# A delta-rule recurrence with an MLP behind it, on one core: the inverse's two PSUM banks lent to the MLP's second product, one weight piece fewer, the last outputs on two queues, and a new planning table

## The chip, the cores and the metric

The kernel runs on one core of a Trainium2 chip. Its time is the device time of one execution in microseconds (us). Of the kernel before, three timed runs are shown, from 648.24 to 648.99 us, with a median of 648.69. One more execution was recorded by the profiler. The engines are named as in the profile: PE multiplies matrices, DVE, ACT and POOL (GpSimd) work on elements, SP issues most transfers. PSUM is the memory that PE writes its products to; here it is eight banks of 512 float32 values in each of 128 partitions.

## The reference

```python
# r, k, v, w, a, b: 4 x 8 x 768 x 40, float32; state: 4 x 8 x 40 x 40, zero at first
for t in range(768):
    y[:, :, t] = einsum('bhd,bhde->bhe', r_t, state)
    Sa = einsum('bhde,bhe->bhd', state, a_t)
    state = state * w_t[:, :, None, :] - einsum('bhd,bhe->bhde', Sa, b_t)
    state = state + einsum('bhd,bhe->bhde', v_t, k_t)
x = y.transpose(0, 2, 1, 3).reshape(3072, 320)
out = (((x @ w1) * (x @ w2)) @ w3) @ w_out        # w1, w2: 320 x 1024, w3: 1024 x 1024, w_out: 1024 x 320
```

The four weights are float64. The kernel gets their bits as pairs of 32-bit words.

## The kernel before, in words

**Chunks.** The 768 tokens are cut into 12 chunks of 64. The chunks depend on each other through the state (`SB`) alone. Inside a chunk the recurrence is solved with matrices: the function `scale` (lines 492 to 533) multiplies the inputs by running products of the decay (`scan` L502, `gt` L515, `gi` L519, `xx` L523, `aa` L512), `causal` multiplies them with each other (PE L551) and leaves the 64 x 64 triangles in `JP` and `lm`, and the triangles of all 32 heads are inverted.

**The inverse.** `solve` (from line 571) takes the 32 x 32 blocks on the diagonal. DVE transposes them into the PSUM tile `ab` of 128 x 1024, which is two banks (L604; for the first two chunks, `MERGED`, only half of it), and inverts them there by some forty products and sums (L630 and L634, tags `so.x`). Two transposes put the result into `TDX` (L690 and L693). For the first two chunks two products on PE (`so.m1`, `so.m2`) stand in for a part of that work. `join` (from line 737) makes the block below the diagonal: an inverse product on PE (`jo.mm1`, L753), four copies by ACT into `JP` (L273, the line of the helper `copy`, which all ACT copies have), a second inverse product (`jo.mm2`, L753), and copies into `TT`.

**The state step.** `rec` works on two batches of a chunk at a time (a pair step). All its products have line 840: `zv`, the state product (`rv,SB`), `zn`, three steps with the inverse and flips that transpose the new state. DVE masks `un` between them (L891) and makes the new state `st` (L896) and the output `y` (L900). `pairs` and `tokens` prepare operands (L792, L816), with a mask on POOL (L801).

**The MLP.** `gather` brings `y` into token order by 12 transfers of SP (L915). `mlp` splits it into a high and a low part (`xs`, L940 on ACT and L943 on DVE). Its first product (tag `m.mm1`, L957) gives x @ w1 and x @ w2, 128 matmuls of 256 columns for a chunk, in groups of eight. ACT copies one (`ga`), DVE multiplies it by the other (L971), and the result is split into `gh` (ACT) and `gl` (L974, POOL or DVE). The second product (tag `m.mm2`, L983) multiplies by w3 @ w_out, which was multiplied out at the start: 48 matmuls of 320 columns in two halves of 128 tokens. Each half fills one bank from the pool of six banks that all of PE's products share. ACT copies it to `o`, and two transfers for each half leave by SP (L992).

**The weights.** `convert` turns a piece of 128 x 1024 float64 values into float32: one transfer, `e` (L394), `mf` (L404), its low word (L408), `sg` (L412) on DVE, two steps on ACT, and the output of the conversion (L415) on DVE or POOL, as a table says. There are 17 pieces: 3 of w_out, 8 of w3, 6 of w1 and w2 in three layers of 128 rows. Since 320 is 2 x 128 + 64, the third layer repeats its 64 rows. ACT copies each of these six to the high part of W (`w.hi`), and `w.lo` (L457) makes the low part.

**The order of the work.** All of this goes to a planner, the class `Order`. Each operation is given with a tag, a due time and the buffers that it takes (`SLOTS` says how many of each there are). `place` puts them on the engines one after another by estimated costs (`OPS`) and due times (`P`, `OFF`, `T0`, `T`): of the operations that could start on an engine within `LOOK` of the first, the one with the earliest due time. On PE `STICK` counts against a change of mode, between products of 128, 64 and 32 rows. `ON` says for some tags whether DVE or POOL does them. The result is a fixed order on each engine, with semaphores between them. When an operation runs on the chip depends on these alone.

**The end.** Behind the last chunk a check of the inputs' range sums `stats`, PE multiplies it by ones (L1098, `good`), DVE makes the flag `bad`, and all engines load it (L1102) and branch on it (L1103). The branch isn't taken with these inputs.

Of the kernel before, what the change touches and what calls it, by code (L numbers as in the profile page):

```python
# [19 lines left out]
NCH = S // C  # L20
# [12 lines left out]
SLOTS = dict(fm=4, xx=3, aa=3, lm=4, gi=1, gt=1, ab=1, TDX=1, rv=4, vg=5, un=4, bk=5, hs=2, st=2, y=1, xr=1, JP=2, TT=2, bank=6,  # L33
# [8 lines left out]
ON = dict(aa="dppddpdddppdpppddppppddd", cv="pdddppdddpddddppp",
          gl="dpppdpppddppddpppdddddpppppdpdpdppppddddpppdpppp", ws="pdddpp", xs="ddpddppppdpppdddppddpdpd")
OFF = {"ca.j": -611.218, "ca.js": -295.116, "ca.lm": -409.432, "ca.mask": 322.878, "ca.mm": -196.496, "cv.e":
       -352.619, "cv.exp": -294.308, "cv.f": 875.871, "cv.in": 923.729, "cv.lo": 148.411, "cv.m": -331.453, "cv.out":
       -690.808, "cv.sign": -986.054, "ga": 652.698, "jo.cp1": 176.7, "jo.cp2": 1171.31, "jo.mm1": 500.308, "jo.mm2":
       559.977, "jo.tt": 1216.266, "ld.aa": 255.685, "ld.fm": -308.122, "ld.xx": -220.769, "m.a": -43.748, "m.ab":
       -25.534, "m.gh": -539.967, "m.gl": -14.3, "m.mm1": 97.143, "m.mm2": 289.0, "m.o": 98.802, "m.out": -533.298,
       "m.xh": -105.084, "m.xl": 349.579, "nil": 390.528, "pa.cp": -142.457, "pa.mask": 411.539, "pa.mm": 399.693,
       "pa.rv": 721.462, "pa.v": -32.743, "r.hs": -489.727, "r.n": 318.043, "r.s": -178.475, "r.sb": -189.193, "r.st":  # L50
       490.608, "r.t0": -269.903, "r.t1": 72.728, "r.t2": -860.309, "r.tr": -475.318, "r.u": -459.283, "r.y":
       -480.807, "r.zn": -15.068, "r.zv": -155.411, "sc.aa": 621.487, "sc.chk": -167.343, "sc.exp": 187.27, "sc.gi":
# [59 lines left out]
class Part:  # L112


    def __init__(self, slot, i):
        self.slot, self.i = slot, i

    @property
    def t(self):
        return self.slot.t[:, self.i * NP:(self.i + 1) * NP]  # L120


class Order:

# [7 lines left out]
    def slot(self, pool):  # L135
        return Slot(self, pool)
# [1039 lines left out]
```

## Time and profile before

| what | value |
|---|---|
| three runs, median (lowest to highest) | 648.69 us (648.24 to 648.99) |
| profiled execution: its own time | 643.84 us |
| its span, first to last instruction | 642.1 us |
| mean granted PE clock | 0.984 |
| busy in the span: PE, DVE, ACT, POOL | 88%, 74%, 60%, 29% |
| bytes moved by DMA | 68.23 MB |

The span is shorter than the execution's own time by what lies around the instructions, 1.74 us. A busy time is the sum of an engine's instructions; an idle time is what is left, and the profile names for it the instruction on another engine (the releaser) whose semaphore came last. PE's float32 matmuls appear twice each in the counts of the trace: an order's `x16` is a trace's `x32`. In the names of tiles the trace leaves the buffer's number out; the orders below show it. In 40 slices of 16 us the page shows a granted clock below 0.9 four times: 0.8, 0.6 and 0.8 between 96 and 177 us, and 0.8 in the last.

### The profile page before, as it was taken

What the parts mean: (1) busy time and instruction counts of PE and PEld (TensorE: products, weight loads), DVE (VectorE), ACT (ScalarE), POOL (GpSimd) and SP (SyncE); (2) the same over time, 40 slices, a digit from 0 to 9 for tenths busy, and PEclk for the clock granted to TensorE, in tenths of its full rate; (3) what the DMA queues carried; (4) which work ended last, traced back from release to release, by engine and by line L of the source; (5) the groups of instructions that cost most, each with busy time, mean ns of one, the idle gap of its engine ahead of it and who ended that gap; (6) DMA issues with size and microseconds to landing.
All of it is one profiled execution on the core that took longest, in us unless ns stands there. A gap on an engine that the chain in (4) does not pass through costs nothing.

```text
span 642.1 us, 27039 instructions
## 1 busy us (share of the span) xinstructions
PE 566.2 (88%) x11970; PEld 503.9 (78%) x11970; DVE 473.3 (74%) x849; ACT 382.5 (60%) x825; POOL 184.7 (29%) x230
## 2 busy tenths in 40 slices
PE   1536889867999999999999999998999999999995
PEld 0435767556988988888888889887988898898995
DVE  6799897987949959769589599497595794971220
ACT  6767557686465665755755746657557557354221
POOL 3542414035332413403312115332232242020111
PEclk9999989968999999999999999999999999999998
DMA  8975566535213423523534335235135333210001
GB/s 193 294 225 167 154 212 217 196 87 152 69 29 85 117 69 98 141 48 90 137 80 110 82 79 134 59 96 141 41 93 141 78 83 81 51 37 14 26 21 25
DMA packets 53401, 68.23 MB, mean 106 GB/s; under 512 B 29984, under 2 KB 37664, under 8 KB 51232
## 3 DMA queue, kind: packets, MB, share of 16 engines
q1 hardware_dynamic: 53280, 66.46, 38.3%
q8 instruction: 95, 1.56, 1.0%
q14 instruction: 26, 0.21, 0.1%
HBM read 57.79 MB, written 3.93 MB: 96 GB/s over the span
## 4 chain that ended last, share of the span: by engine, by line
PE 36%; DVE 28%; ACT 17%; DMA 9%; SPq 5%; issue 4%; POOL 0%; ACTq 0%; DVEq 0%
PE bank L957 15%; PE bank L840 9%; ACT JP L273 5%; DVE tmp L630 4%; SPq L915 4%; DMA fm<-in_fmg_dram 4%; PE bank L983 4%; ACT TT L273 3%; PE bank L551 3%; DMA xr<-y 3%; DVE ab L604 2%; PE bank L470 2%; DVE mf L408 2%; DVE ga L971 2%; ACT hs L273 2%
## 5 line engine op out<-in xcount | busy, mean ns | idle before, releaser
L957 PE MATMUL bank<-xs,W 128*128 128x256 f32 x1536 | 208.3, 288 | 2.8 <-ACT o L273 2.8
L957 PEld LDWEIGHTS bank<-xs,W 128*128 128x128 f32 x1536 | 187.8, 189 | 14.1 <-ACT o L273 3.6
L273 ACT ACTIVATE gh<-ga 128x512 fp32r<-128x512 f32 x48 | 30.3, 631 | 94.8 <-DVE ga L971 94.8
L891 DVE TENSOR_TENSOR un<-bank,mask_h 128x416 f32<-128x416 f32 x48 | 28.2, 588 | 73.0 <-PE bank L840 63.9
L974 POOL TENSOR_TENSOR gl<-ga,gh 128x512 fp32r<-128x512 f32 x29 | 37.5, 1292 | 118.3 <-ACT gh L273 92.4
L801 POOL TENSOR_SCALAR_AFFINE_SELECT vg<-vg 64x256 f32<-64x256 f32 x96 | 43.9, 457 | 74.6 <-DVE gl L974 24.0
L983 PE MATMUL bank<-W3h,gh 128*128 128x320 f32 x192 | 63.8, 332 | 0.0
L567 POOL TENSOR_SCALAR_AFFINE_SELECT lm<-lm 64x512 f32<-64x512 f32 x48 | 34.0, 708 | 95.5 <-ACT lm L273 74.7
L983 PE MATMUL bank<-W3l,gh 128*128 128x320 f32 x192 | 59.2, 308 | 0.0
L983 PE MATMUL bank<-W3h,gl 128*128 128x320 f32 x192 | 59.2, 308 | 0.0
L273 ACT ACTIVATE JP<-bank 64x256 f32<-64x256 f32 (+2 forms) x120 | 45.4, 379 | 20.7 <-PE bank L551 19.0
L840 PE MATMUL bank<-hs,TT 64*64 64x104 f32 x768 | 49.8, 269 | 7.3 <-ACT TT L273 5.2
L840 PE MATMUL bank<-un,bk 64*64 64x104 f32 (+1 forms) x768 | 47.9, 266 | 2.8 <-DVE un L891 2.3
L523 POOL TENSOR_TENSOR xx<-xx,gi 112x1024 f32<-112x1024 f32 x12 | 28.5, 2379 | 74.6 <-DVE gi L519 22.9
L971 DVE TENSOR_TENSOR ga<-bank,ga 128x512 f32<-128x512 f32 x48 | 32.7, 681 | 22.3 <-PE bank L957 22.3
L840 PEld LDWEIGHTS bank<-hs,TT 64*64 64x64 f32 x768 | 39.3, 142 | 11.5 <-ACT TT L273 6.0
L840 PE MATMUL bank<-vg,bk 64*64 64x104 f32 (+1 forms) x768 | 47.1, 264 | 0.0
L840 PEld LDWEIGHTS bank<-un,bk 64*64 64x64 f32 (+1 forms) x768 | 37.8, 130 | 8.9 <-DVE un L891 5.6
L551 PE MATMUL bank<-aa,xx 40*64 40x64 f32 x1536 | 32.8, 239 | 10.7 <-POOL xx L523 5.5
L551 PEld LDWEIGHTS bank<-aa,xx 40*64 40x64 f32 x1536 | 30.5, 153 | 12.9 <-POOL xx L523 5.7
L470 PE MATMUL bank<-wof,w3f 128*128 128x320 f32 x128 | 38.0, 453 | 2.4 <-DVE w3f L415 1.5
L273 ACT ACTIVATE ga<-bank 128x512 f32<-128x512 f32 x48 | 28.7, 597 | 16.9 <-PE bank L957 16.3
(120 smaller groups left out, 1245.9 us busy)
## 6 DMA issues: line engine op xcount, KB each, us to landing
rv<-in_rv_dram SPq DMA_DIRECT2D x48, 294.0 KB
xx<-in_fmx_dram SPq DMA_DIRECT2D x24, 448.0 KB
raw<-in_w3t_dram SPq DMA_DIRECT2D x8, 1024.0 KB
raw<-in_w_dram SPq DMA_DIRECT2D x6, 1024.0 KB
fm<-in_fmg_dram SPq DMA_DIRECT2D x24, 227.5 KB
aa<-in_fma_dram SPq DMA_DIRECT2D x24, 224.0 KB
vg<-in_vt_dram SPq DMA_DIRECT2D x48, 80.0 KB
out_dram<-o SPq DMA_DIRECT2D x48, 80.0 KB
```

What stands on the lines that cost most here:

```text
L273: act.activation(out_, in_, AF.Copy, scale=scale)
L470: pe.matmul(out=pt.t[:, 0:DM], lhsT=w[:, j], rhs=wof[:, j], start=(j == 0), stop=(j == NJ - 1))
L523: e.tensor_tensor(out=X, in0=X, in1=gi.t.unsqueeze(2).to_broadcast([ROWS, 2 * NP, 2, C]), op=ALU.mult)
L551: pe.matmul(out=bank(s)[64 * z:64 * z + 64, i, p], lhsT=X[r, p, z], rhs=aa[i].t[r, p], start=True, stop=True)
L567: op("ca.mask", due + 6, lambda q=q: pool.affine_select(out=lm.t[q], in_=lm.t[q], pattern=[[0, 2 * NP], [1, C]], compare_op=ALU.is_gt, fil ...
L801: op("pa.mask", due + 2, lambda q=q, vg=vg: pool.affine_select(out=vg.t[q, :, 0:C], in_=vg.t[q, :, 0:C], pattern=[[0, NP], [1, C]], compar ...
L840: pe.matmul(out=out_(ab ^ z, p), lhsT=left(ab, ab ^ x, p), rhs=right(ab ^ x, p), start=start and p == 0, stop=True, skip_group_check=True)
L891: dve.tensor_tensor(out=un[i].t, in0=view(hp[i]), in1=mask_h.unsqueeze(1).to_broadcast([128, NP, N]), op=ALU.mult)
L957: pe.matmul(out=pt.t[:, TOK * x:TOK * x + TOK], lhsT=WT[k][:, cs], rhs=xs.t[:, z], start=(n == 0), stop=(n == 7))
L971: op("m.ab", t, lambda a=a, pt=pt: dve.tensor_tensor(out=a.t, in0=wide(pt), in1=a.t, op=ALU.mult), r=[pt], w=[a])
L974: both(("gl", c % NCH * 4 + j // 2), "m.gl", t + 1, lambda e, a=a, j=j: e.tensor_tensor(out=gl.t[:, j:j + 2], in0=a.t, in1=gh.t[:, j:j + 2 ...
L983: pe.matmul(out=pt.t[:, 0:DM], lhsT=l.t[:, j, ts], rhs=W3[r][:, j], start=(j == 0 and n == 0), stop=(j == NJ - 1 and n == 2))
```

## The change

There are four edits.

1. The pool `ab` with one buffer becomes the pool `xb` with two, which are the two halves of `ab`, one bank each. An inverse takes both (for the first two chunks one). The second product of the MLP takes one for each of its halves, in place of a bank from the pool of six.
2. The third layer of w1 and w2, 64 rows, comes as one piece of 128 x 1024 (`wc`: w1's rows above w2's) in place of two pieces with the rows repeated. There are 16 pieces. The two `w.hi` and the two `w.lo` of that layer work on 64 rows each, and both `w.lo` are on DVE.
3. In the last chunk the second transfer of each half (`m.oa`) is issued by ACT, in place of SP.
4. The planner's tables have new numbers: `T0`, `T`, `P`, `ON`, `OFF`, some costs in `OPS` (with a delay for cold transfers and one for their landing, which `place` now adds), `LOOK` and `STICK`.

```diff
-SLOTS = dict(fm=4, xx=3, aa=3, lm=4, gi=1, gt=1, ab=1, TDX=1, rv=4, vg=5, un=4, bk=5, hs=2, st=2, y=1, xr=1, JP=2, TT=2, bank=6,
+SLOTS = dict(fm=4, xx=3, aa=3, lm=4, gi=1, gt=1, xb=2, TDX=1, rv=4, vg=5, un=4, bk=5, hs=2, st=2, y=1, xr=1, JP=2, TT=2, bank=6,
...
-T0, T = 449.562, 122.639
+T0, T = 555.384, 101.503
...
-FLIGHT, QUEUE, STICK = 1.9, 8, 34.913
+FLIGHT, QUEUE, STICK = 1.9, 8, 4.365
...
+class Whole:
+
+
+    def __init__(self, t):
+        self.t = t
...
+    tiles["xb"] = [tiles["ab"][0][:, 512 * i:512 * i + 512] for i in range(2)]
...
-    pieces = iter(range(17))
+    pieces = iter(range(16))
...
-            for f in range(2 * DFF // CW):
+            for f in range(2 * DFF // CW if k < 2 else 1):
                 cs = slice(CW * f, CW * f + CW)
-                mf = convert(w12[k * 128:k * 128 + 128, cs], None, due)
-                n = (0, 1, 4)[k]
-                rows = slice(64, 128) if k == 2 else slice(0, 128)
+                mf = convert(w12[k * 128:k * 128 + 128, cs] if k < 2 else wc, None, due)
                 over = ["conv"] if k == 0 else ["conv", "reg2"]
-
-                def f1(mf=mf, n=n, cs=cs):
-                    copy(WT[n][:, cs], mf.t)
-
-                def f2(e, mf=mf, n=n, rows=rows, k=k, cs=cs):
-                    e.tensor_tensor(out=WT[2 + k][rows, cs], in0=mf.t[rows], in1=WT[n][rows, cs], op=ALU.subtract)
-
-                op("w.hi", due, f1, r=[mf, *over], w=[("W", k, f)])
-                both(("ws", 2 * k + f), "w.lo", due, f2, r=[mf, *over], w=[("W", k, f)])
+                for x in (f,) if k < 2 else range(2):
+                    xs = slice(CW * x, CW * x + CW)
+                    q, z = (slice(0, 128),) * 2 if k < 2 else (slice(64 * x, 64 * x + 64), slice(64 - 64 * x, 128 - 64 * x))
+                    hi, lo = (0, 1, 4)[k], 2 + k
+
+                    def f1(mf=mf, hi=hi, q=q, xs=xs):
+                        copy(WT[hi][q, xs], mf.t[q])
+
+                    def f2(e, mf=mf, hi=hi, lo=lo, q=q, z=z, xs=xs):
+                        e.tensor_tensor(out=WT[lo][z, xs], in0=mf.t[q], in1=WT[hi][q, xs], op=ALU.subtract)
+
+                    op("w.hi", due, f1, r=[mf, *over], w=[("W", k, x)])
+                    if k < 2:
+                        both(("ws", 2 * k + f), "w.lo", due, f2, r=[mf, *over], w=[("W", k, x)])
+                    else:
+                        op("w.lo/d", due, lambda f2=f2: f2(dve), r=[mf, *over], w=[("W", k, x)])
...
-        jp, ab, tdx = jp_[c], slot("ab"), slot("TDX")
+        jp, tdx = jp_[c], slot("TDX")
+        xbs = [slot("xb") for _ in range(1 if c < MERGED else 2)]
+        ab = xbs[0] if c < MERGED else Whole(tiles["ab"][0])
...
-        op(f"so.in/{int(c < MERGED)}", due, s0 if c < MERGED else f0, r=[(jp, "d", 0), (jp, "d", 1)], w=[ab])
+        op(f"so.in/{int(c < MERGED)}", due, s0 if c < MERGED else f0, r=[(jp, "d", 0), (jp, "d", 1)], w=xbs)
...
-            pt, o = slot("bank"), slot("o")
+            pt, o = slot("xb"), slot("o")
...
-                op("m.out", t, lambda b=b, tt=tt, o=o: sp.dma_start(
+                tag, e = ("m.oa", act) if c == NCH - 1 and b else ("m.out", sp)
+                op(tag, t, lambda b=b, tt=tt, o=o, e=e: e.dma_start(
                     out=out[bass.ds((2 * tt + b) * S + row, C)], in_=o.t[64 * b:64 * b + 64]), r=[o])
...
-    rows += rows[256:]
...
-    w12 = bits(np.concatenate([np.asarray(i["moe_w1"])[rows], np.asarray(i["moe_w2"])[rows]], axis=1))
+    w12 = np.concatenate([np.asarray(i["moe_w1"])[rows], np.asarray(i["moe_w2"])[rows]], axis=1)
+    wc = bits(np.concatenate([w12[256:, 0:DFF], w12[256:, DFF:]], axis=0))
+    w12 = bits(w12[:256])
```

The numbers move instructions on every engine. Three places follow. Lines of the changed kernel are higher by 8 to 17: L753 becomes L769, L957 becomes L973, L983 becomes L999, L891 becomes L907, L900 becomes L916, L943 becomes L959, L604 becomes L620, L992 becomes L1009.

PE, chunk 8 (counted from 0) around the second inverse product: `bank_157` is one of the six banks, `ab` the tile of the inverse. Before:

```order
L983 MATMUL bank_157<-W3h,gh_1830 128x320
L983 MATMUL bank_157<-W3l,gh_1830 128x320
L983 MATMUL bank_157<-W3h,gl_1831 128x320
L753 MATMUL bank_154<-TDX_119,JP_144 32x32 x32
L957 MATMUL bank_157<-xs_1832,W_0_100 128x256 x2
L957 MATMUL bank_157<-xs_1832,W_2_101 128x256
```

And in the changed kernel:

```order
L999 MATMUL ab<-W3h,gl_1603 128x320
L769 MATMUL bank_153<-TDX_119,JP_144 32x32 x32
L999 MATMUL ab<-W3h,gh_1602 128x320
L999 MATMUL ab<-W3l,gh_1602 128x320
L999 MATMUL ab<-W3h,gl_1603 128x320
```

Before, twelve rows of the second MLP product stand ahead of the second inverse product, the last of their 48, and first-half products of the next MLP take over their bank right behind it. In the changed kernel 18 stand ahead of it, back to the first inverse product, and 18 more of the same 48 behind it, all in `ab`.

DVE, ahead of the first MLP's input (`xs_1832` before, `xs_1604` in the change, made by L943 and L959). Before:

```order
L630 TENSOR_TENSOR tmp<-GP,ab 128x196
L634 TENSOR_REDUCE GP<-tmp 128x4x7
L891 TENSOR_TENSOR un_131<-bank_158,mask_h 128x416
L891 TENSOR_TENSOR un_132<-bank_157,mask_h 128x416
L900 TENSOR_TENSOR y_142<-bank_155,fm_105 104x4x64
L900 TENSOR_TENSOR y_142<-bank_156,fm_105 104x4x64
L896 TENSOR_TENSOR st_140<-bank_155,fm_105 104x160
L896 TENSOR_TENSOR st_141<-bank_156,fm_105 104x160
L657 TENSOR_TENSOR tmp<-GP 128x128
L943 TENSOR_TENSOR xs_1832<-xr_143,xs_1832 128x768
```

And in the changed kernel:

```order
L533 SCALAR_TENSOR_TENSOR gi_117<-gt_118,gi_117 112x512
L537 TENSOR_TENSOR xx_107<-xx_107,gi_117 112x1024
L468 TENSOR_TENSOR W_4_1202<-mf_167,W_4_1202 64x1024
L907 TENSOR_TENSOR un_129<-bank_157,mask_h 128x416
L468 TENSOR_TENSOR W_4_1202<-mf_167,W_4_1202 64x1024
L907 TENSOR_TENSOR un_130<-bank_154,mask_h 128x416
L959 TENSOR_TENSOR xs_1604<-xr_143,xs_1604 128x768
L916 TENSOR_TENSOR y_142<-bank_156,fm_106 104x4x64
L916 TENSOR_TENSOR y_142<-bank_155,fm_106 104x4x64
L620 STREAM_TRANSPOSE ab<-JP_144 128x1024
```

Before, fifteen steps of the third inverse (L630, L634, L657) and the masks, `y` and `st` of the second chunk's first pair step (L891 to L896) stand ahead of it. In the changed kernel the transpose that begins the third inverse (L620) stands behind it, and two low parts of W (L468, which was L457, of 64 rows each) stand right ahead of it.

ACT, the end of the last chunk: `o` is the output of one half, `bad` the flag. Before:

```order
L273 ACTIVATE gh_1830<-ga_1834 128x512
L273 ACTIVATE o_1835<-bank_156 128x320
L273 ACTIVATE o_1836<-bank_158 128x320
L1102 TENSOR_LOAD bad
L1103 COMPARE_AND_BRANCH
```

And in the changed kernel:

```order
L281 ACTIVATE gh_1602<-ga_1606 128x512
L281 ACTIVATE o_1607<-ab 128x320
L1009 DMA out_dram<-o_1607 64x320
L281 ACTIVATE o_1608<-ab 128x320
L1009 DMA out_dram<-o_1608 64x320
L1119 TENSOR_LOAD bad
```

Two transfers of the output now stand on ACT, each behind the copy that it sends, and the load of the flag behind both.

## Rows read from the trace of the kernel before

**Rows 1.** The page, part 1: busy us, share of the span, instructions.

```profile
PE 566.2 (88%) x11970; PEld 503.9 (78%) x11970; DVE 473.3 (74%) x849; ACT 382.5 (60%) x825; POOL 184.7 (29%) x230
```

**Rows 2.** By stretches: us, busy by engine, PE clock, DMA share, GB/s.

```profile
0.00:158.00 158.00, 102.04 (x2353) 80.68 (x2354) 134.17 (x207) 107.49 (x198) 57.66 (x71) 0.95 0.65 190
457.00:502.00 45.00, 43.32 (x964) 39.08 (x965) 34.20 (x67) 27.69 (x65) 11.98 (x16) 1.00 0.37 94
```

**Rows 3.** PE in order of time: start us, us, operation, idle before.

```profile
157.86 0.51 PE L957 MATMUL bank<-xs,W 128*128 128x256 f32 x2
...
434.71 0.39 PE L983 MATMUL bank<-W3h,gh 128*128 128x320 f32 x1
...
446.08 0.75 PE L753 MATMUL bank<-TDX,JP 32*32 32x32 f32 x64
...
449.53 0.75 PE L753 MATMUL bank<-TDX,JP 32*32 32x32 f32 x64 [0.73 <-ACT JP L273]
```

**Rows 4.** Waits of PE, 180 to 636 us: total us, times, longest.

```profile
PE bank L753 <- ACT JP L273: 4.5, 7, 0.8
PE bank L957 <- ACT o L273: 2.8, 6, 1.0
PE bank L840 <- ACT un L273: 2.0, 4, 1.1
```

**Rows 5.** DVE in order of time, columns as in rows 3.

```profile
143.02 1.99 DVE L604 STREAM_TRANSPOSE ab<-JP 128x1024 f32<-128x1024 f32 x1
...
149.28 0.36 DVE L634 TENSOR_REDUCE GP<-tmp 128x28 f32<-128x196 f32 x1
...
441.46 0.69 DVE L634 TENSOR_REDUCE Tp<-tmp 128x64 f32<-128x512 f32 x1
...
453.34 0.59 DVE L891 TENSOR_TENSOR un<-bank,mask_h 128x416 f32<-128x416 f32 x1 [6.93 <-PE bank L840]
...
457.22 2.04 DVE L604 STREAM_TRANSPOSE ab<-JP 128x1024 f32<-128x1024 f32 x1 [1.53 <-ACT JP L273]
...
487.43 0.68 DVE L693 STREAM_TRANSPOSE TDX<-TDX 128x512 f32<-128x512 f32 x1
```

**Rows 6.** DVE by line and form: count, busy us, mean ns, idle before.

```profile
L408 DVE SCALAR_TENSOR_TENSOR mf<-raw,mf 128x1024 f32<-128x1024 uint32 x16 | 21.2, 1326 | 0.2
...
L900 DVE TENSOR_TENSOR y<-bank,fm 104x256 f32<-104x256 f32 x48 | 17.8, 410 | 6.1 <-PE bank L840 5.9
...
L523 DVE TENSOR_TENSOR xx<-xx,gi 112x1024 f32<-112x1024 f32 x12 | 14.4, 1202 | 0.1
...
L404 DVE TENSOR_SCALAR mf<-raw 128x1024 int32<-128x1024 int32 x16 | 11.4, 715 | 1.1 <-DMA raw<-in_w3t_dram 1.0
...
L415 DVE TENSOR_TENSOR w3f<-mf,sg 128x1024 f32<-128x1024 f32 x6 | 7.3, 1222 | 0.2
```

**Rows 7.** PE in order of time, a pair step's products, as rows 3.

```profile
430.22 0.59 PE L840 MATMUL bank<-ident,st 40*40 40x40 f32 x32
...
440.18 0.94 PE L840 MATMUL bank<-vg,lm 64*64 64x104 f32 x32
440.94 0.90 PE L840 MATMUL bank<-rv,SB 40*40 40x104 f32 x32
```

**Rows 8.** The chain that ended last: start us, us, what.

```profile
587.51 1.14 PE bank L957 x8
...
613.07 15.24 PE bank L957 x128
628.32 7.06 PE bank L983 x48
```

**Rows 9.** Lines 992, 1103, 1172: ns min/median/max, first to last start us.

```profile
L992 SPq DMA_DIRECT2D out_dram<-o x8: 466/554/597, 610.4 to 636.4; - x8
...
L1103 SPq EVENT_SEMAPHORE  x8: 17/17/17, 639.8 to 640.4; - x8
...
L1172 SPq EVENT_SEMAPHORE  x10: 17/28/28, 640.4 to 642.1; - x10
```

More of the change, by code (lines that the diff above doesn't have):

```diff
@@ L42 @@
[L42 to L52, printed above, removed]
-       -148.615, "sc.gt": -230.551, "sc.ln": 87.006, "sc.scan": 203.673, "sc.xs": 130.059, "so.d": -775.834, "so.in":
-       -264.37, "so.m1": -358.78, "so.m2": -299.304, "so.q": 713.223, "so.sa": -515.229, "so.sb": -535.393, "so.t":
-       -345.96, "so.td": 366.095, "so.tt": -385.449, "so.v": -186.183, "so.x": -90.021, "so.z": 257.847, "tk.cp":
-       -717.729, "tk.mm": 348.057, "w.hi": 667.696, "w.lo": -164.398, "w3.hi": 386.505, "w3.lo": -443.484, "w3.mm":
-       -484.2, "z.bk": 434.685}
@@ L65 @@
     "w3.mm": ("pe", 2.15, 0, "128", 2.33, 16, 0.838, 1.88), "w3.hi": ("act", 0.44), "w3.lo": ("dve", 0.46),
-    "ld.fm": ("sp", 0.42, 0, None, 0.85), "ld.xx": ("sp", 0.42, 0, None, 1.85), "ld.aa": ("sp", 0.42, 0, None, 0.85),
-    "sc.chk": ("act", 0.64), "sc.scan": ("dve", 1.26, 1), "sc.ln": ("act", 0.62), "sc.exp": ("act", 0.76),
+    "ld.fm": ("sp", 0.42, 0, None, 0.75, 0, 0.3, 0.5), "ld.xx": ("sp", 0.42, 0, None, 1.85, 0, 0.3, 0.85), "ld.aa": ("sp", 0.42, 0, None, 0.88, 0, 0.3, 0.4),
+    "sc.chk": ("act", 0.73), "sc.scan": ("dve", 1.26, 1), "sc.ln": ("act", 0.62), "sc.exp": ("act", 0.63),
@@ L73 @@
     "so.m2": ("pe", 1.26, 0, "32", 1.42, 256, 0.179, 1.45), "so.t": ("act", 0.4),
[L74 to L76 removed]
+    "jo.mm1": ("pe", 0.58, 0, "32", 0.75, 128, 0.1, 1.45), "jo.cp1": ("act", 0.375), "jo.mm2": ("pe", 0.58, 0, "32", 0.75, 128, 0.1, 1.45),
@@ L77 @@
+    "jo.cp2": ("act", 0.375), "jo.tt": ("act", 0.625),
+    "pa.rv": ("sp", 0.42, 0, None, 1.08, 0, 0.3, 0.6), "pa.v": ("sp", 0.65, 0, None, 0.36, 0, 0.3, 0.4), "pa.mm": ("pe", 0.52, 0, "64", 0.66, 64, 0.089, 1.88), "pa.cp": ("act", 0.4),
     "pa.mask": ("pool", 0.42, 1),
@@ L238, in place @@
             elif e == "sp":
-                done, clock[e] = max(t + FLIGHT, landed[-1]) + o["span"], t + o["cost"]
+                done, clock[e] = max(t + FLIGHT + o["cold"], landed[-1]) + o["span"], t + o["cost"]
                 landed.append(done)
+                done += o["act"]
             else:
@@ L261, in attention_moe @@
 @with_exitstack
-def attention_moe(ctx: ExitStack, tc: tile.TileContext, fmg, fmx, fma, rv, vt, sq, svr, w12, w3t, wo, out):
+def attention_moe(ctx: ExitStack, tc: tile.TileContext, fmg, fmx, fma, rv, vt, sq, svr, w12, wc, w3t, wo, out):
     nc = tc.nc
@@ L707, in solve @@
         for cost, fn, two in steps:
-            op("so.x", t, fn, r=[ab], w=["solve"], cost=cost, two=two)
+            op("so.x", t, fn, r=xbs, w=["solve"], cost=cost, two=two)
             t += cost * span / total
@@ L1158, in _layout @@
     return {n: np.ascontiguousarray(t) for n, t in
-            dict(fmg=fmg, fmx=x, fma=fma, rv=rv, vt=vt, sq=sq, svr=svr, w12=w12, w3t=w3t, wo=wo).items()}
+            dict(fmg=fmg, fmx=x, fma=fma, rv=rv, vt=vt, sq=sq, svr=svr, w12=w12, wc=wc, w3t=w3t, wo=wo).items()}
 def kernel(**inputs):
```

41 lines of the change are left out of this document (27 added, 14 removed).

## Prediction

> **What bounds the kernel now.** I read the busy shares first [rows 1]: the tensor engine (PE) works for 88% of the span, the vector engine (DVE) for 74%. An average hides where each of them rules, so the table by stretches comes next [rows 2]. In the first stretch, to 158 us, DVE is busy for 134.17 of 158.00 us and PE for 102.04. In a stretch of one chunk later PE is busy for 43.32 of 45.00 and DVE for 34.20. So there are two kernels in one: a front, in which weights are converted and the first states computed, set by DVE, and from 158 us on a part set by PE. The border is the first product of the MLP at 157.86 [rows 3], right behind the DVE instruction that makes its second input.
>
> In the second part PE waits little. The list of its waits between 180 and 636 us [rows 4] names 4.5 us for JP copies and 2.8 for copies of o; the next is 2.0 for un. The first kind sits ahead of the second product of the inverse, at 449.53 with 0.73 us [rows 3]: twelve products of the MLP's second half stand between the two inverse products, and the four copies between them take longer. The second kind sits ahead of an MLP product that takes over the bank which the copy of o must empty first.
>
> DVE has two phases in a chunk of the second part [rows 5]. From 457.22, where an inverse begins, to 488.11, where its last transpose ends, it hardly stops; ahead of 457.22 it waits, 6.93 us of it in one piece for a product of PE. The next inverse can't start before PE has done both inverse products, the step behind them and the next chunk's causal product. That is a loop through both engines of some 44 us, and PE is nearly full in it: both are close to being the bound.
>
> **The change, part by part.** *Front.* One conversion of a weight piece goes, and the order puts other work ahead of the first MLP product. I counted both orders on DVE up to the instruction that makes its input, and priced the difference [rows 6]. Gone are e, mf, sg (three at about 0.715) and the low word (1.326) of one piece, 3.5 us; two outputs of conversions that GpSimd takes, 2 x 1.222; two masks, priced like mf, 1.4; four y and four st, priced like y, 8 x 0.410 = 3.3; and the first fifteen steps of the third inverse, from 143.02 to 149.64 [rows 5] less 0.6 for an sg among them, 6.0. In come three more low parts of W, 3 x 1.222, two aa priced like mf, 1.4, and one xx, 1.2. That is 16.6 less and 6.3 more: 10.3 us less. But PE does less as well before its first MLP product, and owes it afterwards: two zv, two state products, one zn, two flips, three steps with the inverse, eight transposes and sixteen rv. By the rows [rows 7], with zn and the steps priced like a state product and the last two items like a flip each, that is 2 x 0.94 + 2 x 0.90 + 4 x 0.90 + 2 x 0.59 + 2 x 0.59 = 9.6 us. DVE's part comes 10.3 earlier and PE is 9.6 behind: **the front is worth nothing**, 0. That holds if DVE idles as now, 158.00 - 134.17 = 23.8 us. The bounds are a fifth of that, 5 us either way.
>
> *Middle.* The MLP's second product moves into the two banks of the inverse. It can no longer run while an inverse is being computed, as it does now: it began at 434.71 [rows 3] when DVE worked on that inverse until 442.15 [rows 5]. Of its 48 products 36 stood ahead of the first inverse product; now 6 do, with 24 in most chunks between the two inverse products and 18 behind. Two waits lose their ground. Behind 24 products of 7.06 / 48 = 0.147 us [rows 8], 3.5 us, the JP copies are done; and an MLP product no longer needs a bank that waits for o. That is 4.5 + 2.8 = 7.3 us. By my count of the order PE also changes between wide and narrow products 250 times from the first MLP product on, against 264. Eight products alone take 1.14 us, as a sixteenth of a dense run 15.24 / 16 = 0.95 [rows 8], so entering and leaving cost 0.19 and fourteen changes 1.3. Together 8.6.
>
> The loop must allow it. From one inverse's first product to the start of the next inverse it is 457.22 - 446.08 = 11.1 us [rows 3, 5]. There 30 products of 0.147 come in and 16 first-half products of 15.24 / 128 = 0.119 go out: 4.4 - 1.9 = +2.5. Inside the inverse DVE has in most chunks one scan, one gt, one ga and one to two gl fewer, and mostly one xx more: with the scan priced like xx and the others like mf [rows 6] -1.2 - 0.7 - 0.7 - 1.0 + 0.8 = -2.8. With the 0.73 of the lost wait the loop gets 1.0 us shorter per chunk, 9.0 in nine: just enough for 8.6. As it is that close I take **-7.0**. The ends: -10.6 if the 2.0 for un go as well (9.3 + 1.3), and 0 if the loop gives nothing.
>
> On such banks the Trainium skill ("PSUM — Partial Sum Buffer", section "PSUM bank collisions raise a hardware error") says that two engines must never be in one bank of a partition at the same time, and that the chip does not arbitrate. By that page the second product has to stand behind the whole inverse, which gives the first rival below; the trace of before, with separate banks, can't show it.
>
> *End.* The last chunk's outputs go out half by SP, half by ACT. SP issues the last of them at 636.4, 0.554 us each in the median, waits for landings from 639.8 on, and the program ends at 642.1 [rows 9]. With one DMA on each queue the last starts 0.55 sooner; the flag's product moves twelve products forward and drops out of the end. **-0.5**; the bounds are 0 and two issues, -1.1.
>
> The Trainium skill ("DMA: Bandwidth & Descriptors", section "Issuing engines are not separate DMA queues") says that a second issuing engine only saves the time to initiate a DMA. By it the term is the issue and nothing of the landing; a gain of the 3.4 us from issue to landing would go against it. No run here shows a transfer from ACT yet.
>
> *At nothing* I cost the removed piece's DMA and its copies on ACT: ACT is busy for 107.49 of 158.00 us in the front [rows 2], DVE covers it.
>
> **Sum.** 0 - 7.0 - 0.5 = -7.5 us. The profiled execution took 643.84, 1.74 more than its span, so 636.3 is expected of it. The median shown is 648.69, 4.85 above that execution; with the same difference I predict **641.2 us**.
>
> **Rivals.** *The inverse's loop lengthens.* DVE waits inside the inverse for masks and y, which hang on PE; then moving 2.8 us of other work out doesn't shorten it, and the +2.5 stays. It decides as soon as less than 1.8 of the 2.8 is gained (2.5 - 0.73). With 1.0 gained it costs 0.8 a chunk, 7 in nine, less 0.5 at the end: 655.2; with nothing gained 1.8 a chunk, 664. Against it: DVE runs that stretch now nearly without a stop. Chance 0.12. *The front loses.* The second chunk's inverse starts far later in DVE's order, behind most of the weights; if DVE meets its long chain PE, copy, PE, copy with nothing to do, 5 us of idle time come in, and with only -3 in the middle and the end at -0.5 it is 650.2. Against it: order alone adds no work. Chance 0.08. *No change:* the waits for JP and o go but others as long come, masks above all, which PE now meets behind short covers: 0 - 0.5, 648.2. Chance 0.10. *Both gain:* the front sheds 5 of its 23.8 us of idle time and the middle gives 10: 648.69 - 15.5 = 633.2. Chance 0.15; for it, the idle time is there. That leaves 0.55 for the forecast.
>
> **How the numbers follow.** About 0.2%, 1.3 us, is what a measurement can tell from no change. Faster is forecast and double gain, 0.55 + 0.15 = 0.70; same 0.10; slower 0.12 + 0.08 = 0.20. The range, 633 to 652, takes in the double gain, the forecast with 5 either way in the front, no change and the late front; it leaves out the loop's 0.12 and the outer end of the gain.
>
> **What would show it.** Right: the first MLP product near 148 us; no wait for JP ahead of the second inverse product and none of a first-half product for o; chunks some 0.8 us shorter than 44; the last outputs issued singly. Wrong: DVE's 6.93 us of idle time ahead of the mask shrinking to nothing while PE waits at L999 or L769 for the inverse; then the loop is the bound. A first MLP product after 152 us would break the front's step.

## The result, and the profile after

The changed kernel takes 623.91 us, median of 4 runs (623.41 to 626.09), against 648.47 (647.37 to 648.99) for the kernel before in the same comparison. The ratio is 0.963, 95% interval 0.9604 to 0.9656. That is 24.6 us less. I had forecast 7.5 less, and the measured time lies below my range. In all medians here and below, executions more than 1.5% above the fastest of their kernel in the same comparison are left out.

The page's busy times and granted clock of the changed kernel, to be held against [rows 1]:

```profile
PE 552.3 (89%) x11970; PEld 497.4 (80%) x11970; DVE 471.0 (76%) x843; ACT 384.9 (62%) x823; POOL 179.4 (29%) x231
...
PEclk9999999959999999999999999999999999999999
```

PE does the same number of instructions, and its busy time is 13.9 us shorter. Where the 19.7 us between the two spans (642.1 and 622.4) lie is read from four stretches with borders that both traces have: the first product of the MLP, the start of the fourth inverse, the start of the twelfth, the end. Columns as in [rows 2]; before first, then after.

```profile
0.00:157.90 157.90, 101.94 (x2353) 80.58 (x2353) 134.07 (x207) 107.40 (x197) 57.66 (x71) 0.95 0.65 190
157.90:194.10 36.20, 34.84 (x602) 32.85 (x600) 25.65 (x43) 22.60 (x48) 12.50 (x12) 1.00 0.24 60
194.10:545.40 351.30, 340.95 (x7675) 308.06 (x7675) 273.97 (x522) 220.28 (x512) 102.16 (x132) 1.00 0.37 95
545.40:642.10 96.70, 88.47 (x1350) 82.41 (x1349) 39.65 (x79) 32.25 (x69) 12.35 (x15) 0.98 0.12 29
```

```profile
0.00:141.20 141.20, 86.34 (x1993) 67.64 (x1993) 119.38 (x179) 98.11 (x177) 42.06 (x61) 0.94 0.63 190
141.20:184.20 43.00, 41.57 (x960) 38.19 (x958) 35.85 (x66) 28.82 (x67) 14.74 (x18) 1.00 0.38 98
184.20:527.40 343.20, 335.69 (x7716) 308.25 (x7720) 275.59 (x523) 224.93 (x514) 113.33 (x141) 1.00 0.38 97
527.40:622.40 95.00, 88.72 (x1318) 83.27 (x1308) 40.23 (x77) 33.06 (x67) 9.22 (x12) 0.99 0.12 31
```

The first product comes 16.7 us earlier (157.9 to 141.2); from there to the fourth inverse it takes 6.8 longer (36.2 to 43.0); eight chunks from the fourth to the twelfth inverse take 8.1 less, 1.0 each; and the end takes 1.7 less. So the front, to the fourth inverse, gained 9.9, the middle 8.1 and the end 1.7.

The medians differ by 4.9 more than the spans. The executions of the kernel before spread, and in part with their granted clock: in the four later comparisons of this study, those with a mean clock of 0.983 or more took 644.0 us on average (10 of 60), those from 0.977 to 0.982 took 646.8 (40), those below 648.5 (10). The profiled one had 0.984 and was short for its kernel. The four runs of the changed kernel all lie at 0.983 to 0.985. Against executions of a like clock the change is worth about 20 us. The other 4 to 5 go along with the lower clock of most executions of the kernel before; that the clock alone makes them isn't shown.

PE's waits from 160 to 616 us in the changed kernel, columns as in [rows 4]:

```profile
PE bank L856 <- DVE un L907: 2.6, 6, 0.9
PE bank L973 <- ACT ga L281: 1.9, 5, 0.5
PE bank L769 <- DVE TDX L709: 1.7, 6, 0.4
...
PE ab L999 <- ACT o L281: 0.9, 2, 0.5
...
PE bank L769 <- ACT JP L281: 0.3, 1, 0.3
```

The wait for the JP copies ahead of the second inverse product fell from 4.5 to 0.3, and no first-half product waits for `o` any more. Three others came or grew: for masks (before 0.5), for `ga` (none listed before) and for the inverse itself (`TDX`, before 0.3).

### The profile page after: what moved, and what is told of

It reads as the page before. It is cut to its first block, busy times and chain, and to the rows that moved or that the text cites. A ratio compares the mean times of both kernels' runs of the same rounds, so it can differ in the third digit from the quotient of the medians.

```text
span 622.4 us, 27016 instructions
## 1 busy us (share of the span) xinstructions
PE 552.3 (89%) x11970; PEld 497.4 (80%) x11970; DVE 471.0 (76%) x843; ACT 384.9 (62%) x823; POOL 179.4 (29%) x231
## 4 chain that ended last, share of the span: by engine, by line
DVE 40%; PE 38%; ACT 12%; issue 5%; DMA 2%; POOL 1%; SPq 1%; ACTq 0%; DVEq 0%; POOLq 0%
PE ab L999 12%; PE bank L973 11%; DVE tmp L646 9%; PE bank L856 8%; ACT JP L281 3%; DVE ab L650 3%; PE bank L769 2%; PE bank L565 2%; DVE ga L987 2%; DVE fm L516 2%; DVE Tp L650 2%; DVE GP L650 2%; DVE ab L620 2%; PE bank L484 1%; DVE y L916 1%
## 5 line engine op out<-in xcount | busy, mean ns | idle before, releaser
L973 PE MATMUL bank<-xs,W 128*128 128x256 f32 x1536 | 210.9, 288 | 3.0 <-ACT ga L281 1.9
L973 PEld LDWEIGHTS bank<-xs,W 128*128 128x128 f32 x1536 | 188.6, 189 | 11.3 <-ACT ga L281 2.5
L990 POOL TENSOR_TENSOR gl<-ga,gh 128x512 fp32r<-128x512 f32 x32 | 42.4, 1324 | 149.3 <-ACT gh L281 117.6
L999 PE MATMUL ab<-W3h,gh 128*128 128x320 f32 x192 | 62.4, 325 | 0.9 <-ACT o L281 0.9
L999 PE MATMUL ab<-W3h,gl 128*128 128x320 f32 x192 | 59.3, 309 | 0.0
L999 PE MATMUL ab<-W3l,gh 128*128 128x320 f32 x192 | 59.2, 308 | 0.0
L817 POOL TENSOR_SCALAR_AFFINE_SELECT vg<-vg 64x256 f32<-64x256 f32 x96 | 40.6, 423 | 46.8 <-ACT vg L281 16.6
L907 DVE TENSOR_TENSOR un<-bank,mask_h 128x416 f32<-128x416 f32 x48 | 28.2, 587 | 32.6 <-PE bank L856 32.5
L856 PE MATMUL bank<-un,bk 64*64 64x104 f32 (+1 forms) x768 | 45.5, 256 | 3.2 <-DVE un L907 2.8
L537 POOL TENSOR_TENSOR xx<-xx,gi 112x1024 f32<-112x1024 f32 x10 | 24.2, 2421 | 62.7 <-DVE gi L533 40.5
L856 PE MATMUL bank<-vg,lm 64*64 64x104 f32 x768 | 23.3, 260 | 19.5 <-POOL vg L817 19.5
L832 PE MATMUL bank<-ident,xx 104*128 104x104 f32 x192 | 27.9, 273 | 14.2 <-POOL xx L537 14.2
```

The source lines that it names most:

```text
L817: op("pa.mask", due + 2, lambda q=q, vg=vg: pool.affine_select(out=vg.t[q, :, 0:C], in_=vg.t[q, :, 0:C], pattern=[[0, NP], [1, C]], compar ...
L856: pe.matmul(out=out_(ab ^ z, p), lhsT=left(ab, ab ^ x, p), rhs=right(ab ^ x, p), start=start and p == 0, stop=True, skip_group_check=True)
L907: dve.tensor_tensor(out=un[i].t, in0=view(hp[i]), in1=mask_h.unsqueeze(1).to_broadcast([128, NP, N]), op=ALU.mult)
L973: pe.matmul(out=pt.t[:, TOK * x:TOK * x + TOK], lhsT=WT[k][:, cs], rhs=xs.t[:, z], start=(n == 0), stop=(n == 7))
L990: both(("gl", c % NCH * 4 + j // 2), "m.gl", t + 1, lambda e, a=a, j=j: e.tensor_tensor(out=gl.t[:, j:j + 2], in0=a.t, in1=gh.t[:, j:j + 2 ...
L999: pe.matmul(out=pt.t[:, 0:DM], lhsT=l.t[:, j, ts], rhs=W3[r][:, j], start=(j == 0 and n == 0), stop=(j == NJ - 1 and n == 2))
```

## The experiments

### Parts undone or exchanged, and the planner runs again

Four kernels cross the parts of the change. In each the planner's table decides anew about the order.

```diff
 # new_structure_old_numbers: changed kernel, T0, T, P, ON, OFF, LOOK, OPS, STICK of before
 # old_structure_new_numbers: kernel before, the same of the changed kernel; of both, one line is shown, for the second:
-T0, T = 449.562, 122.639
+T0, T = 555.384, 101.503
 # mm2_in_six_banks: changed kernel
-            pt, o = slot("xb"), slot("o")
+            pt, o = slot("bank"), slot("o")
 # seventeen_pieces: changed kernel, the whole of edit 2 taken back; ON gets letters for the new operations
-    pieces = iter(range(16))
+    pieces = iter(range(17))
```

> The changed kernel's buffers, pieces and queues with the planner's numbers of before. If the two banks themselves free PE from its waits, the 8 us that the middle gained are here too: about 640. If the gain is the order that the new numbers make, and the banks only allow it, nothing is gained or the order, whose numbers were set for other buffers, is worse: 645 to 665.

> The buffers, 17 pieces and one queue of before with the planner's numbers of the changed kernel (a 17th letter for the conversions, two more for the low parts). If the order alone moves the front, the fourth inverse starts near 184 us as in the changed kernel, and about 10 us are gained: 638. If the front needs the dropped piece, it starts 3.5 us later, 188. If the middle needs the two banks, chunks stay near 44 us there.

> The changed kernel, with the MLP's second product back in a bank of the pool of six. If the banks make the middle, it loses the 8 us there: 632. If the order makes it, the time stays within 3 us of 624. The front, where only one second product lies, should stay.

> The changed kernel with 17 pieces, the third layer again in two pieces with its rows repeated. DVE gets 3.5 us more in the front. If DVE sets the front, the time is 3.5 to 5 us longer, 627.5 to 629; if PE or a chain of waits sets it, it stays within 1 us of 624.

The stretches are from the one trace of each kernel, in us.

| kernel | median | ratio, interval | first MLP product | fourth inverse | fourth to twelfth | end |
|---|---|---|---|---|---|---|
| before | 646.36 | 1 | 157.9 | 194.1 | 351.3 | 96.7 |
| changed | 623.91 | 0.963 (0.960 to 0.966) | 141.2 | 184.2 | 343.2 | 95.0 |
| new_structure_old_numbers | 688.66 | 1.066 (1.056 to 1.077) | 146.9 | 185.9 | 408.1 | 95.5 |
| old_structure_new_numbers | 667.88 | 1.037 (1.027 to 1.046) | 151.4 | 191.5 | 358.0 | 112.4 |
| mm2_in_six_banks | 648.77 | 1.005 (1.002 to 1.008) | 141.5 | 185.8 | 354.1 | 107.6 |
| seventeen_pieces | 670.17 | 1.039 (1.029 to 1.049) | 151.8 | 190.1 | 358.9 | 119.3 |

The totals missed every expectation: each part undone loses some 25 us or more. Numbers set for one structure make a bad order for another. In the two with banks and numbers that don't belong together the inverse waits for the copy of `o`, the MLP's output that still lies in its banks. DVE's waits from 180 to 600 us, new_structure_old_numbers and seventeen_pieces (total us, times, longest):

```profile
DVE ab L620 <- ACT o L281: 43.1, 7, 10.1
```

```profile
DVE ab L615 <- ACT o L281: 35.3, 7, 11.5
```

In the changed kernel no such wait is listed. In mm2_in_six_banks PE's wait for the JP copies is back instead, 5.7 us from 160 to 600 us. So these totals price no part. The first columns do say something. With 16 pieces the fourth inverse starts near 184 to 186, with old numbers or new, with the two banks or without; with 17 pieces it starts at 190 to 194. The cleanest pair is seventeen_pieces and the changed kernel, which have the same numbers: 190.1 against 184.2, and the first MLP product at 151.8 against 141.2. As expected, the fourth inverse stays near its place when the second product goes back to six banks (185.8). And without the two banks no order got the middle under 351; with them two of three are longer still (358.9 and 408.1), so the banks alone don't do it.

### The numbers searched anew for each structure

To price the parts, three structures got numbers of their own, searched by the planner's own estimate from those of the changed kernel on; `OPS` stays that of the changed kernel.

```diff
 # refit_17_pieces: seventeen_pieces; refit_six_banks: mm2_in_six_banks; refit_old_structure: old_structure_new_numbers
 # in each T0, T, P, ON, OFF, LOOK, STICK anew, as in refit_six_banks:
-T0, T = 555.384, 101.503
+T0, T = 649.356, 134.510
```

> The changed kernel with 17 pieces again, as in the run with seventeen pieces, but with planner numbers searched anew for it by the planner's own estimate, starting from those of the changed kernel. If the piece itself is worth only its 3.5 us of DVE, as the prediction priced it, 627 to 629; if it is worth what the unfitted run lost, 670. The fourth inverse starts later than in the changed kernel by the piece's part of the front, 3 to 7 us.

> The changed kernel with the second MLP product in the pool of six banks, with numbers searched anew for it. The front stays, with the fourth inverse near 184. If the two banks are worth the middle's gain as forecast, 7 us, about 631; if the whole of the unfitted run's loss, 649.

> Buffers, pieces and the one queue of before, with numbers searched anew, starting from those of the changed kernel. If the numbers of before were as good as this structure allows, 645 or more. If order alone can bring a part of the gain, 632 to 642; what is left to 624 is then the worth of piece, banks and queue together.

| kernel | median | ratio, interval | first MLP product | fourth inverse | fourth to twelfth | end |
|---|---|---|---|---|---|---|
| before | 646.57 | 1 | 157.9 | 194.1 | 351.3 | 96.7 |
| refit_17_pieces | 637.78 | 0.985 (0.978 to 0.992) | 155.7 | 190.9 | 350.9 | 95.6 |
| refit_six_banks | 638.80 | 0.986 (0.978 to 0.994) | 140.7 | 185.7 | 358.9 | 91.4 |
| refit_old_structure | 647.82 | 1.003 (0.999 to 1.008) | 148.7 | 194.5 | 359.7 | 91.9 |

New numbers alone bring nothing here: the old structure stays where it was. The dropped piece without the banks brings 8 us and the banks without the dropped piece 9 (by the intervals 4 to 14, each with the second queue), and both 23 to 25. The two expectations of 627 to 631 were too low: without the banks 15 us are lost, without the dropped piece 14. These are upper bounds, because the search behind them was short. None of the runs is faster than the changed kernel. The front follows the number of pieces again (190.9 and 194.5 against 185.7). That the middle with 17 pieces isn't at 343, though it has the banks, goes with its inverses' waits for `o`, 14.3 us on DVE in seven pieces; whether a better order could avoid them with 17 pieces, the runs don't tell.

The longest of them, DVE in order of time at the start of the fourth inverse:

```profile
190.92 1.98 DVE L600 STREAM_TRANSPOSE ab<-JP 128x1024 f32<-128x1024 f32 x1 [7.96 <-ACT o L266]
```

The inverse waits 7.96 us for that copy. In the changed kernel the same start waits 1.81 us, for JP.

### The front, with the order held

Six kernels keep the order of their base row for row and take away or shift one piece of work, so that the planner can't mix in.

```diff
 # before_lows_on_dve: kernel before
-                    e.tensor_tensor(out=WT[2 + k][rows, cs], in0=mf.t[rows], in1=WT[n][rows, cs], op=ALU.subtract)
+                    (dve if k == 2 else e).tensor_tensor(out=WT[2 + k][rows, cs], in0=mf.t[rows], in1=WT[n][rows, cs], op=ALU.subtract)
 # after_lows_on_pool: changed kernel
-                        op("w.lo/d", due, lambda f2=f2: f2(dve), r=[mf, *over], w=[("W", k, x)])
+                        op("w.lo/d", due, lambda f2=f2: f2(pool), r=[mf, *over], w=[("W", k, x)])
 # before_piece_left_out: kernel before, convert() of the last piece (f1 too: before_piece_and_transfer_out)
+            f2 = f3 = f4 = f5 = f6 = f7 = lambda: None
+            f8 = lambda e: None
 # before_step_left_out: kernel before, in rec's product() (with the piece: before_step_and_piece_left_out)
+            if c == 1 and gs[0] == 0:
+                return
```

> The kernel before in its own order, but the two low parts of W's third layer are made by DVE in place of POOL, where they were its last work ahead of the MLP: 147.94 to 152.84 us. If that chain on POOL set the first MLP product, it comes 3 to 5 us earlier, near 154, and the fourth inverse as much earlier. If DVE's work sets it, it comes 2.4 us later, 160.

> The kernel before in its own order; the conversion of the last of the 17 pieces is left out on DVE, ACT and POOL (its transfer and the copies from its old buffer stay). DVE does 3.5 us less, POOL 2.1. If DVE sets the front, the first MLP product comes 3.5 us earlier, 154.4; if the chain piece, POOL, low parts sets it, 2 to 5; if PE's pair steps of chunk 1 set it, it stays within 1 of 157.9. Behind it, if PE is full and owes nothing, the whole program ends as much earlier.

> The changed kernel in its own order, but POOL makes the two low parts of the third layer. If their chain sets the first MLP product (135.67 to 138.76 on DVE), two of 2.35 in place of two of 1.22 us put it 2.3 to 4 us later, 143.5 to 145; if DVE's work sets it, it comes 2.4 us earlier. The end of the program moves by as much if the stretch behind it is full, by less if it has slack.

> The kernel before in its own order; the products of chunk 1's second pair step are left out on PE (its copies, masks and outputs stay). They are 9 us of PE's busy time at most, and stand from 143.8 to 156.4 us ahead of the first MLP product. If DVE sets the front, that product stays within 2 us of 157.9. If PE, walking in its order through a step that waits for ACT and DVE, sets it, it comes 8 to 12 us earlier, 146 to 150, up to where the weights are ready (152.8 on POOL, or earlier since POOL waits less).

> The same with the conversion of the last of the 17 pieces left out as well. If with the step gone the weights are what the first MLP product waits for, it comes 3 to 5 us earlier than with the step alone; alone, the piece had moved it by less than 2 us. If not, the two runs agree within 2 us.

> The kernel before in its own order, with the last piece's conversion and its transfer of 1 MB left out. Without its conversion alone the way from the second inverse product of chunk 1 to the first MLP product stayed at 28.7 us against 28.3. If the transfer held that way up, it is 3 to 5 us shorter, 24; if it is the order on PE, 28 again.

Executions differ by some 2 us ahead of the place, so I measure from the start of chunk 1's second inverse product to the first MLP product. PE's idle time and its granted clock on this way are from the same traces.

| kernel | from | to | us | PE idle | PE clock |
|---|---|---|---|---|---|
| before | 129.53 | 157.86 | 28.3 | 8.0 | 0.76 |
| before_lows_on_dve | 130.52 | 161.36 | 30.8 | 8.2 | 0.67 |
| before_piece_left_out | 130.90 | 159.57 | 28.7 | 7.5 | 0.72 |
| before_piece_and_transfer_out | 128.82 | 158.99 | 30.2 | 7.7 | 0.67 |
| before_step_left_out | 131.92 | 159.56 | 27.6 | 12.2 | 0.62 |
| before_step_and_piece_left_out | 128.83 | 155.89 | 27.1 | 11.6 | 0.63 |
| changed | 130.73 | 141.16 | 10.4 | 1.8 | 0.61 |
| after_lows_on_pool | 130.51 | 141.47 | 11.0 | 1.6 | 0.53 |

The medians of the kernels on the order of before were 646.30 to 650.73, with ratios of 0.999 to 1.006; after_lows_on_pool took 624.62. DVE's theory fell: 3.5 us less of DVE's work (the piece) moved nothing. POOL's chain fell: taking the low parts off it made nothing shorter, and putting them on it in the changed kernel cost 0.5. The transfer fell as well. And PE's step alone fell, which I had thought would settle it. The 2.5 us by which the low parts on DVE lengthen the way look like the 2.4 that DVE's theory gave, but PE idles no longer there: its 625 products are busy 2.3 us longer, at a clock of 0.67 in place of 0.76. With the piece and its transfer left out the clock is 0.67 as well, and the way 1.9 longer. So differences of 2 us between these single traces say nothing about the edits. Why nothing came of leaving PE's step out stands in the trace of before_step_left_out, PE and POOL in order of time:

```profile
152.44 0.48 PE L792 MATMUL bank<-rv 40*64 40x64 f32 x4 [6.79 <-DMA rv<-in_rv_dram]
...
156.48 1.76 PE L842 MATMUL bank<-vg,lm 64*64 64x104 f32 x32 [1.08 <-POOL vg L801]
```

```profile
153.09 2.35 POOL L457 TENSOR_TENSOR W<-mf,W 64x1024 fp32r<-64x1024 f32 x1 [0.46 <-ACT W L273]
155.51 2.16 POOL L801 TENSOR_SCALAR_AFFINE_SELECT vg<-vg 64x256 f32<-64x256 f32 x3
```

With the step gone PE stands 6.79 us for a load of `rv`, then for a mask that POOL makes behind the last low part. So behind the one way to the first MLP product there stood others that end within 2 us of it, and leaving out one leaves them. That the search for the order had made them so fits, but no run shows it.

What the order does is seen in stretches (columns as in [rows 2]). First the way of the table and what follows it up to the fourth inverse, before and after:

```profile
129.53:157.86 28.33, 20.36 (x625) 17.41 (x625) 22.13 (x41) 19.36 (x38) 13.73 (x12) 0.76 0.39 111
157.86:194.10 36.24, 34.88 (x603) 32.89 (x600) 25.69 (x43) 22.60 (x48) 12.50 (x12) 1.00 0.24 60
```

```profile
130.73:141.16 10.43, 8.60 (x260) 7.61 (x261) 5.62 (x7) 8.36 (x17) 4.46 (x3) 0.61 0.06 11
141.16:184.19 43.03, 41.60 (x960) 38.22 (x959) 35.88 (x65) 28.85 (x67) 14.74 (x18) 1.00 0.38 98
```

Some 360 products of PE, as the trace counts them, moved from ahead of the first MLP product to behind it. On the way they took 17.9 us, 11.8 busy and 6.1 idle; behind it they take 6.8, 6.7 of it busy. Ahead of the way the number of products is the same (1729 and 1732), and it starts 1.2 us later. 17.9 - 6.8 - 1.2 is the front's gain of 9.9. Then the kernel before from the end of that inverse product to the first MLP product, and the 25 us behind the first MLP product in the changed kernel:

```profile
130.30:157.86 27.56, 19.61 (x561) 16.77 (x561) 21.36 (x41) 19.36 (x38) 12.96 (x12) 0.75 0.38 104
```

```profile
141.20:166.00 24.80, 24.50 (x491) 22.59 (x492) 24.08 (x52) 14.40 (x34) 8.32 (x13) 1.00 0.39 100
```

Before, two pair steps of chunk 1 stand there with nothing to cover them. PE is busy for 19.61 of 27.56 us at a granted clock of 0.75, DVE for 21.36: no engine is full. On the page of the kernel before the low slices of the clock lie at 80 to 96 us, at 128 to 161 and at the end, not between 96 and 177 as I had written; those from 128 to 161 hold this stretch. The changed kernel has its low slice, 0.5, from 124 to 140 us, with fewer products in it. These are PE's longer waits in that stretch:

```profile
133.97 0.60 PE L840 MATMUL bank<-hs,TT 64*64 64x104 f32 x2 [3.68 <-ACT TT L273]
...
146.24 1.34 PE L840 MATMUL bank<-un,aa 40*64 40x104 f32 x32 [0.75 <-ACT un L273]
149.11 0.31 PE L840 MATMUL bank<-hs,TT 64*64 64x104 f32 x2 [1.53 <-ACT hs L273]
150.80 0.43 PE L840 MATMUL bank<-un,bk 64*64 64x104 f32 x2 [0.76 <-DVE un L891]
...
155.74 0.69 PE L840 MATMUL bank<-ident,st 40*40 40x40 f32 x30 [0.62 <-DVE st L896]
```

In the changed kernel the second of the two steps (its flips at 164.28) runs inside the MLP's first product. Its masks, `y` and `st` are those ahead of `xs_1832` in the order of before, which I had put to the first step. PE is busy for 24.50 of 24.80 us at a clock of 1.00, and its only wait in that window is 0.30 us, for `xs`. The weights are early enough for that: the last piece's transfer is issued at 113.06, where before the last four take from 113.37 to 128.01.

```profile
113.37 14.64 SPq L391 DMA_DIRECT2D raw<-in_w_dram  x4
```

```profile
113.06 0.35 SPq L400 DMA_DIRECT2D raw<-in_wc_dram  x1
```

### The wait for the JP copies, with the order held

```diff
 # before_one_jp_copy: kernel before; three of the four copies between the inverse products are left out
-                op("jo.cp1", due + 1, lambda b=b, h=h, ns=ns: copy(
+                op("jo.cp1", due + 1, lambda b=b, h=h, ns=ns: b and h and copy(
```

> The kernel before in its own order; of the four copies between the two inverse products only one is made. If PE's waits for them cost what the list of waits says, 4.5 us go between 180 and 636 us, and about 3 more in the front, where the second chunk's product waited 3.58 us: 636 in the profile's time against 643.8. If the loop through DVE takes the time back, the fourth to the last inverse stay 351 us apart and the gain is under 2.

638.68 us median against 646.27; ratio 0.982, interval 0.975 to 0.989. From the fourth to the twelfth inverse the profiled execution took 350.7, as before, but that is two things. By stretch (before_one_jp_copy; the kernel before took 263.10 and 88.20 between the same inverses):

```profile
192.40:451.00 258.60, 255.77 (x5755) 231.18 (x5755) 204.34 (x390) 158.55 (x367) 76.66 (x99) 1.00 0.38 98
451.00:543.10 92.10, 87.40 (x1923) 78.50 (x1922) 68.78 (x134) 52.72 (x122) 25.33 (x33) 0.98 0.32 87
```

Six chunks gained 4.5 us at full clock, where the list gives 3.2 for JP copies and 1.4 for `o`, whose waits went too. Two then lost 3.9: PE waits there 2.1 us in one piece for `un` and 1.4 for `aa`, with a clock of 0.98. So the run met one half of each expectation: a gain of 7.6, and inverses still 351 us apart. In six chunks the waits were worth what the list says; whether the loop through DVE took it back in the last two, or that execution's clock, one trace doesn't tell.

### The end

```diff
 # one_queue: changed kernel, its order held
-                tag, e = ("m.oa", act) if c == NCH - 1 and b else ("m.out", sp)
+                tag, e = ("m.oa" if c == NCH - 1 and b else "m.out"), sp
```

> The changed kernel in its own order, but SP issues all outputs. The last matmul ended 4.8 us before the end of the span in the changed kernel, 6.7 before. If the second queue makes that difference, its end is 1.9 us later: 625.8 against 623.9, and 6.7 us behind the last matmul. By the term of the prediction 0.5 to 1.1. If the flag's product, which stands earlier in both, made it, no change.

624.55 us median against 623.91 of the changed kernel, ratio to before 0.962 (0.954 to 0.970). The last matmul ended 6.65 us ahead of the end of the span before, 4.83 in the changed kernel, and 5.58 here. The second queue is worth 0.8. The other 1.1 is put down to the flag: before, SP loads it behind its last transfer, here ahead of it. No run moves the flag alone, and in the other traces on the order of before that tail is 6.4 to 7.0. The rows of SP, before and in one_queue, whose last transfers are issued at 636.4 and 618.7:

```profile
L1102 SPq TENSOR_LOAD <-bad x1: 737/737/737, 637.0 to 637.0; - x1
```

```profile
L1119 SPq TENSOR_LOAD <-bad x1: 922/922/922, 616.8 to 616.8; - x1
```

## Why the prediction was wrong

**The front, the step that failed.** "DVE's part comes 10.3 earlier and PE is 9.6 behind: the front is worth nothing." DVE began the input of the first MLP product 15.3 us earlier (156.13 to 140.81), the product itself came 16.7 earlier, and PE's debt was 6.8: a gain of 9.9. The condition that DVE idles as now nearly held: up to that input its idle time fell from 23.8 to 21.8. Its busy time fell by 13.3, 3.0 more than I had counted. But DVE's sum isn't the mechanism: DVE's 134.17 of 158.00 us [rows 2] were an average over a front whose last 27.56 us were set by no engine, and taking 3.5 us from DVE there moved nothing. I counted busy time and not how long the moved work stood on PE. It had stood in a stretch with 7.95 us of PE idle and a clock of 0.75, and took 17.9 us there; behind the MLP's start the same number of products takes 6.8, at full clock and with next to no waits. My bound of 5 us either way, a fifth of DVE's idle time, was taken from the wrong engine.

What goes with that order is the dropped piece, which I priced at its 3.5 us of DVE. In the orders that the planner made anew, 16 pieces in place of 17 moved the fourth inverse by 6 to 9 us (184.2 to 185.9 with 16 pieces, 190.1 to 194.5 with 17); in the held order leaving its conversion out moved nothing. Both hold in these runs; how the piece lets the planner move the step, and how its share divides between DVE, ACT, POOL and the loads, stays open.

**The middle, nearly right in size, not in its parts.** Forecast -7.0, measured -8.1. The two named waits went as forecast, from 6.3 us between the fourth and the twelfth inverse to none that is listed, and six chunks of the JP run agree with their listed size. But PE's idle time there fell only from 10.4 to 7.5, because waits for masks, `ga` and `TDX` came in their place. The other 5.3 us are busy time, where I had 1.3 for mode changes. Most of that is waits that a row hides. PE's groups by line between the fourth and the twelfth inverse, before and after:

```profile
L840 PE MATMUL bank<-un,aa 40*64 40x104 f32 x512 | 18.9, 257 | 2.2 <-ACT un L273 2.0
...
L840 PE MATMUL bank<-ident,st 40*40 40x40 f32 x512 | 10.5, 207 | 0.0
```

```profile
L856 PE MATMUL bank<-un,aa 40*64 40x104 f32 x512 | 15.1, 255 | 0.0
...
L856 PE MATMUL bank<-ident,st 40*40 40x40 f32 x517 | 8.5, 206 | 0.0
```

The same products of nearly the same mean length are 3.8 and 2.0 us shorter in all; the other groups change both ways and take back 0.5. The product with `un` and `aa` serves both batches, interleaved. It starts when the first copy of `un` is there, and stands inside for the second. Of the 1.34 us in the row at 146.24 above four products fall into the first 0.40; the fifth begins at 146.65, when the second copy has ended:

```profile
145.69 0.91 ACT L273 ACTIVATE un<-bank 104x416 f32<-104x416 f32 x2
```

Where both copies are ready the row takes 0.94. Before, 13 of its 22 rows take 1.19 us or more; in the changed kernel one does, at 121.86, where the granted clock is 0.5. The profile books this wait as busy.

**The banks.** The second product stands behind the whole inverse, as forecast. Behind the inverse of chunk 8 its first matmul begins at 426.01, and DVE's last read of `ab` (begun at 424.88, 0.69 long) ends at 425.57. That agrees with the Trainium skill ("PSUM — Partial Sum Buffer", section "PSUM bank collisions raise a hardware error"), by which two engines must not meet in a bank. The kernel's buffers enforce that order, so no run here shows what a meeting would do. The rival made of it, a longer loop, didn't come: chunks are 42.9 us long on average, against 43.9. But kernels whose order doesn't fit show a form of it, inverses that wait for `o`: 43.1, 35.3 and 14.3 us in three of them.

**The end.** Forecast -0.5 with bounds 0 and -1.1; the queue gave 0.8. The flag, which I moved out of the end and priced at nothing, goes with the other 1.1. On the queue the measured 0.8 lies between one issue (0.53 us in the median) and two, far from the 3.4 from issue to landing; that agrees with the Trainium skill ("DMA: Bandwidth & Descriptors", section "Issuing engines are not separate DMA queues").

**The rivals and the signs.** "Both gain" (5 from the front, 10 from the middle, 633.2) came nearest, but its front was half the size and came from DVE's idle time, which fell by 2.0 only. What I had listed: the first product near 148 (it was 141.2, on the good side), the JP wait gone (0.3 left), chunks 0.8 shorter (1.0), outputs singly (issued at 615.5 and 618.1 on both queues). Of the 17.3 us between forecast and measured time the front has 9.9, the middle 1.1, the end 1.2 and the medians 4.9: I carried the profiled execution's distance from its median over to the changed kernel, whose clock varies less. And the 1.3 us that I took for the noise were too few: the kernel before spread from 641.1 to 651.7 us.

## What to carry to other kernels

Ask of a moved step not how long it is busy but how long it stands there, idle time and clock included, and what will lie beside it at its new place; a front with no full engine is priced by elapsed time. In this kernel, whose order was fitted by search, removing one thing with the order held showed nothing, and undoing one thing with the planner free showed too much. If ways that end together and numbers that no longer fit are the reasons, as I think, other fitted kernels will do the same: to price a part, fit the order again for each structure, and read parts from stretches of the trace. Where a product consumes two copies in turn, look at the longest and shortest of its rows: the difference is a wait that the list of waits doesn't have.

## What was not expected of the hardware

The mean granted clock of one kernel's executions varies from 0.969 to 0.985, with times from 641.1 to 651.7 us (60 executions of the kernel before), while twelve executions on the changed order stay between 0.982 and 0.986 and 623.4 to 626.1 us. With work of PE left out the clock was lower: the medians of eight executions each were 0.972 for before_step_left_out and 0.973 for before_step_and_piece_left_out, against 0.979 for the kernel before in the same comparison, at about the same time. In the profiled execution of the first PE idles 6.79 us at one place.
